# First weights fetched from ScalarE's queue, padded unit rows, weight decode in four steps, and a new order of the first ten units

## The chip, the cores and the metric

One NeuronCore of a Trainium2 chip runs the whole kernel. The metric is the device time of one execution in microseconds; lower is better. Before the change, three runs took 793.53, 794.27 and 796.66 us, a median of 794.27 us.

## What the kernel computes

Three stages follow each other. The first is a linear attention with a decaying state (batch 4, 8 heads, 768 steps, head size 48):

```python
for t in range(S):
    cur = np.einsum('bhd,bhe->bhde', u[None] * kt, vt)
    y[:, :, t] = np.einsum('bhd,bhde->bhe', rt, state + cur)
    state = wt[:, :, :, None] * state + np.einsum('bhd,bhe->bhde', kt, vt)
```

Its output is read as 3072 tokens of 384 numbers. The second stage is a dense layer with a softmax gate and a norm; the third a dense layer with a leaky maximum:

```python
h = x @ w_in                                   # 384 -> 1024
solu = h * softmax(h)
ln = (solu - mean) / sqrt(var + 1e-6) * g_ln
x = ln @ w_out                                 # 1024 -> 384
g = max(0.01 * h2, h2), h2 = x @ w2_in         # 384 -> 2048
out = g @ w2_out                               # 2048 -> 384
```

The four weight matrices and the norm's gain arrive as 64-bit floats; the attention's inputs are rounded to 32 bits on the host, which also lays them out.

## The kernel before

The 3072 tokens are cut into 24 **units** of 128 tokens. For each unit the attention is done chunk-wise: VectorE (DVE in the profile) makes running products of the decay with two scans (`prep1`, L379, into `suf`; `prep3`, L397, into `e`), scales the transposed keys and queries (`prep_k` L390 gives `kt`, `prep4` L406 gives `lt`), and TensorE (PE) makes the products (`att_scores` L447, `att_u` L467, `att_y` L510 and L519). `att_x` (L525, L526) sums the result on DVE, `x_t` transposes it, `x_hi` on ScalarE (ACT) and `x_lo` (L540) on DVE split it into a rounded high part and a low rest. `mm1` (L548) multiplies it by `w_in` in three passes of nine matmuls in each half. `soft_max` (L553, the row maximum), `soft_e`, `soft_z`, `soft_nm`, `soft_c`, `soft_q` and `z_t`, `z_hi`, `z_lo` make the gated vector and split it. `mm2` (L601) multiplies by `w_out`, four units behind.

Each unit has two tiles from memory: `tr` (112 rows of 1545 floats: decay, keys, queries; two buffers, so the fetch for unit i waits until unit i-2 is used up) and `natq` with `natv` (keys, queries and values by token). All are fetched by SyncE's queue (SP), in program order. A fetch whose buffer isn't free yet therefore holds up all that stand behind it.

Before `mm1` of unit 0 can run, the 64-bit `w_in` must be **decoded** into two 32-bit matrices. It is cut into six blocks of 128 by 512 (three rows of blocks in two halves), and `w_out` into eight of 128 by 384. For each block, `w1_a` takes the exponent (DVE, L111, then ACT, L113), and `w1_b` does four DVE instructions in a row: sign (L119), top bits (L121), sum (L123), product (L125). `w1_c` rounds the block on ACT (L671) and subtracts on PE (L673, L674, through the one PSUM tile `PO`); `w1_d` copies the rest from `PO` on ACT (L680). `w1_c` and `w1_d` of successive blocks share `PO` and so follow each other. The blocks of `w_in` are staged in the buffers `zh` (first half) and `zl` (second half) by `load_i`, and those of `w_out` by `load_o` in the second buffer of each name.

The order of all this is written out by hand: a table `FIRST` names every step of units 0 to 9 and of the decode, in the order in which the steps are issued, and each engine takes its own instructions in that order. From unit 10 on, a loop table `LOOP` repeats for each unit. After the units, the third stage runs (L763, L787). Its weights are decoded in the last part of the units and after them.

Of the kernel before, what the change touches and what calls it, by code (L numbers as in the profile page):

```python
# [35 lines left out]
prep1 2; att_mid 1; prep_diag 1; prep2 2; att_evac_s 1; att_mul_next 1; att_state 1; w1_a; prep_state 2; prep_k 2;
prep3 2; load_i 1; prep_check 1; w1_b; w1_a; att_kt 2; prep4 2; w1_a; w1_c; w1_d; w1_b; w1_c; w1_a; w1_b; w1_d;
w1_c; w1_a; load_o 0; w1_d; mm1 0 0; w1_a; prep_vd 1; w1_b; w1_c; load_tr 3; prep_check 2; w1_d; load_tr 4; w1_b;
att_y 1; load_nat 2; prep_bonus 2; w1_c; w1_b; w1_d; w1_a; w1_a; w1_c; w1_a; w1_a; w1_d; w1_b; w1_b; mm1 0 1; prep1
3; att_evac_k 2; soft_max 0; att_x 1; x_t 1; att_u 2; w1_b; soft_e 0; att_scores 2; w1_c; x_hi 1; att_mid 2; soft_z  # L40
0; soft_nm 0; prep_check 3; load_o 1; w1_d; att_evac_s 2; soft_c 0; soft_q 0; x_lo 1; prep2 3; att_mul_next 2; prep3
3; mm1 1 0; w1_c; w1_d; w1_c; w1_b; w1_a; w1_a; w1_d; prep_k 3; z_t 0; prep4 3; w1_b; load_nat 3; z_hi 0 0; att_kt
3; prep1 4; mm1 1 1; att_evac_k 3; z_lo 0 0; z_hi 0 1; prep_diag 2; prep_vd 2; w1_c; z_lo 0 1; att_state 2; att_y 2;
soft_max 1; load_tr 5; att_u 3; att_x 2; att_scores 3; w1_d; prep_bonus 3; soft_e 1; x_t 2; w1_c; load_nat 4; prep_k
4; att_mid 3; soft_z 1; x_hi 2; prep_check 4; prep_bonus 4; x_lo 2; att_kt 4; att_mul_next 3; soft_nm 1; mm1 2 0;
w1_d; soft_c 1; att_evac_s 3; prep2 4; prep3 4; w1_a; w1_b; prep4 4; mm1 2 1; z_t 1; soft_q 1; z_hi 1 0; w1_b;
att_evac_k 4; prep_diag 3; att_state 3; prep_state 3; z_lo 1 0; w1_c; z_hi 1 1; z_lo 1 1; prep_vd 3; att_scores 4;
prep_state 4; prep_check 5; att_u 4; att_y 3; soft_max 2; prep1 5; w1_d; prep_state 5; att_x 3; w1_c; soft_e 2;
soft_z 2; prep_k 5; x_t 3; att_kt 5; soft_nm 2; x_hi 3; x_lo 3; mm1 3 0; prep2 5; soft_c 2; w1_d; prep3 5; w1_a; z_t
2; att_evac_s 4; mm1 3 1; prep_diag 4; w1_b; z_hi 2 0; att_mid 4; load_nat 5; z_lo 2 0; att_evac_k 5; z_hi 2 1;  # L50
prep4 5; att_mul_next 4; z_lo 2 1; w1_c; load_tr 6; att_scores 5; prep_check 6; load_tr 7; w1_d; att_state 4;
prep_bonus 5; load_nat 6; soft_max 3; prep1 6; att_y 4; prep2 6; prep_vd 4; att_x 4; prep_diag 5; att_u 5; mm2a 4;
soft_q 2; soft_e 3; att_evac_s 5; soft_z 3; prep_state 6; prep_k 6; att_mid 5; x_t 4; x_hi 4; x_lo 4; soft_nm 3;
mm2b 4; prep_bonus 6; prep3 6; att_mul_next 5; att_state 5; mm1 4 0; prep_vd 5; mm2_out 4; soft_c 3; att_kt 6; prep4
6; z_t 3; soft_q 3; mm1 4 1; z_hi 3 0; load_nat 7; load_tr 8; z_hi 3 1; z_lo 3 0; att_scores 6; z_lo 3 1; att_evac_k
6; soft_max 4; att_u 6; att_y 5; prep_diag 6; prep_bonus 7; att_mid 6; att_mul_next 6; prep1 7; mm2a 5; att_x 5;
soft_e 4; att_evac_s 6; x_t 5; prep_k 7; prep2 7; mm2b 5; prep_check 7; soft_z 4; prep1 8; soft_nm 4; x_hi 5; x_lo
5; soft_c 4; mm1 5 0; z_t 4; prep3 7; att_kt 7; z_hi 4 0; prep4 7; prep_diag 7; prep_k 8; mm1 5 1; z_lo 4 0; z_hi 4
1; att_scores 7; prep_vd 6; prep2 8; att_state 6; z_lo 4 1; prep_vd 7; att_y 6; att_evac_k 7; soft_max 5; soft_q 4;
mm2_out 5; prep_check 8; att_u 7; prep3 8; att_kt 8; load_nat 8; att_x 6; soft_e 5; soft_z 5; x_t 6; prep_state 7;  # L60
x_hi 6; soft_nm 5; soft_c 5; mm2a 6; att_mid 7; att_evac_k 8; x_lo 6; mm1 6 0; att_mul_next 7; prep_state 8; z_t 5;
mm2b 6; load_tr 9; z_hi 5 0; z_hi 5 1; load_nat 9; prep1 9; att_state 7; mm2_out 6; z_lo 5 0; att_evac_s 7; mm1 6 1;
prep4 8; prep_check 9; soft_q 5; z_lo 5 1; soft_max 6; prep_bonus 8; att_y 7; soft_e 6; att_scores 8; att_u 8;
prep_diag 8; att_x 7; prep_k 9; prep_bonus 9; att_kt 9; soft_z 6; prep2 9; load_tr 10; soft_nm 6; prep3 9; x_t 7;
x_hi 7; mm2a 7; soft_c 6; x_lo 7; att_mid 8; prep_diag 9; mm1 7 0; prep_vd 8; prep_vd 9; soft_q 6; load_nat 10;
prep4 9; att_mul_next 8; z_t 6; z_hi 6 0; att_evac_k 9; att_evac_s 8; z_lo 6 0; mm1 7 1; prep1 10; prep_k 10; z_hi 6
1; mm2b 7; att_kt 10; z_lo 6 1; soft_max 7; soft_e 7; prep_state 9; prep2 10; att_y 8; prep_bonus 10; att_state 8;
soft_z 7; soft_nm 7; att_scores 9; att_x 8; att_u 9; att_mid 9; load_tr 11; x_t 8; prep_check 10; mm2_out 7; soft_c
7; prep3 10; x_hi 8; x_lo 8; mm2a 8; mm1 8 0; att_mul_next 9; z_t 7; prep_diag 10; prep4 10; z_hi 7 0; soft_q 7; mm1
8 1; att_evac_k 10; prep1 11; prep_state 10; z_hi 7 1; prep_k 11; prep2 11; mm2b 8; att_evac_s 9; z_lo 7 0; z_lo 7  # L70
1; att_state 9; att_scores 10; soft_max 8; att_y 9; load_nat 11; mm2_out 8; att_x 9; att_u 10; soft_e 8; att_kt 11;
x_t 9; x_hi 9; att_evac_k 11; soft_z 8; mm2a 9; soft_nm 8; x_lo 9; prep_bonus 11; mm1 9 0; soft_c 8; att_mid 10;
prep_vd 10; prep_check 11; att_mul_next 10; load_tr 12; att_evac_s 10; load_nat 12; z_t 8; prep_diag 11; z_hi 8 0;
prep1 12; prep_vd 11; prep_state 11; mm1 9 1; prep_check 12; prep_k 12; prep3 11; soft_q 8; prep_bonus 12; att_state
10; z_lo 8 0; z_hi 8 1; prep4 11; z_lo 8 1; mm2b 9; load_tr 13; mm2_out 9; prep2 12
# [39 lines left out]

def decode_val(nc, q, t, dst, scale=2.0 ** -20):
    dve = nc.vector
    hw, lw = q[:, :, 1], q[:, :, 0]
    dve.scalar_tensor_tensor(out=t, in0=hw, scalar=-2147483648, in1=t,  # L119
                             op0=ALU.bitwise_and, op1=ALU.bitwise_or)  # L120
    dve.tensor_scalar(out=hw, in0=hw, scalar1=0xFFFFF, scalar2=0x100000,  # L121
                      op0=ALU.bitwise_and, op1=ALU.bitwise_or)
    dve.scalar_tensor_tensor(out=f(lw), in0=lw.bitcast(U32), scalar=2.0 ** -32, in1=hw,  # L123
                             op0=ALU.mult, op1=ALU.add)
    dve.scalar_tensor_tensor(out=dst, in0=f(lw), scalar=scale, in1=f(t),  # L125
                             op0=ALU.mult, op1=ALU.mult)
# [898 lines left out]
```

## Time and profile before

| | |
|---|---|
| median of three runs | 794.27 us |
| the profiled execution | 794.06 us |
| its span in the trace | 792.4 us |
| PE busy | 735.5 us (93%) |
| DVE busy | 524.3 us (66%) |
| ACT busy | 355.4 us (45%) |
| POOL busy | 166.2 us (21%) |

The busy shares are means over stages of different kinds. The chain of work that ended last gives 65% of the span to PE and 22% to DVE. The span in 40 slices, of 19.8 us each, shows where PE is not full: in the first nine slices, and again around 340 to 500 us, where the third stage's weights are decoded.

### The profile page before, as it was taken

The numbers are of one execution on the slowest core, as the hardware profiler recorded it, in microseconds if no ns is written. First come the engines' busy times: TensorE is split into PE (matmuls) and PEld (weight loads), VectorE is DVE, ScalarE is ACT, GpSimd is POOL, SyncE is SP. The second block draws the span as 40 slices with busy tenths as digits, with TensorE's granted clock in tenths as the row PEclk, the third lists the DMA queues.
The fourth block names the chain that finished last, engine by engine and source line by source line (L and its number), as shares of the span: only waits on it lengthen the run. The fifth ranks groups of instructions, "written<-read, shape, count | busy, mean of one in ns | idle before, by whom it ended". The sixth has DMA issues, their size and how long they took to land.

```text
span 792.4 us, 14979 instructions
## 1 busy us (share of the span) xinstructions
PE 735.5 (93%) x6197; PEld 614.0 (77%) x6197; DVE 524.3 (66%) x866; ACT 355.4 (45%) x648; POOL 166.2 (21%) x181
## 2 busy tenths in 40 slices
...
GB/s 198 251 176 66 67 141 113 145 76 152 134 93 180 118 161 87 12 81 130 91 129 169 80 81 60 1 122 39 0 1 81 0 1 41 0 1 41 0 1 43
DMA packets 31261, 66.60 MB, mean 84 GB/s; under 512 B 4188, under 2 KB 16628, under 8 KB 31060
## 3 DMA queue, kind: packets, MB, share of 16 engines
...
## 4 chain that ended last, share of the span: by engine, by line
PE 65%; DVE 22%; ACT 4%; DMA 4%; issue 3%; POOL 1%; SPq 0%; DVEq 0%; ACTq 0%; POOLq 0%
PE acc L787 19%; PE h L763 18%; PE PH L548 9%; PE PO L601 9%; DMA tr<-in_trw_dram 2%; DVE t L771 2%; PE PZ L510 2%; PE PZ L578 2%; ACT gh L772 2%; DVE w2s L123 2%; DVE w2t L119 2%; DVE gw L777 1%; DVE w2s L121 1%; PE PA L447 1%; PE PZ L519 1%
## 5 line engine op out<-in xcount | busy, mean ns | idle before, releaser
L771 DVE TENSOR_TENSOR t<-t,h 128x512 f32<-128x512 f32 x96 | 65.8, 686 | 122.1 <-ACT t L770 122.1
L763 PE MATMUL h<-x2h,w2ih 128*128 128x512 f32 x288 | 114.5, 397 | 8.1 <-DVE t L771 8.0
L770 ACT ACTIVATE t<-h 128x512 f32<-128x512 f32 x96 | 57.3, 597 | 134.7 <-PE h L763 134.7
L777 DVE TENSOR_TENSOR gw<-t,gh 128x512 fp32r<-128x512 f32 x96 | 69.4, 723 | 66.2 <-ACT gh L772 66.2
L787 PE MATMUL acc<-gh,w2oh 128*128 128x512 f32 x288 | 113.0, 392 | 0.0
L787 PE MATMUL acc<-gw,w2oh 128*128 128x512 f32 x288 | 112.6, 391 | 0.0
L787 PE MATMUL acc<-gh,w2ol 128*128 128x512 f32 x288 | 112.5, 391 | 0.0
L763 PE MATMUL h<-x2l,w2ih 128*128 128x512 f32 x288 | 112.4, 390 | 0.0
L763 PE MATMUL h<-x2h,w2il 128*128 128x512 f32 x288 | 112.2, 390 | 0.0
L772 ACT CAST gh<-t 128x512 fp32r<-128x512 f32 x96 | 59.9, 624 | 95.3 <-DVE t L771 95.3
L754 POOL TENSOR_TENSOR x2l<-x2l,x2h 128x1536 fp32r<-128x1536 f32 x4 | 14.0, 3506 | 297.8 <-ACT x2h L750 297.8
L763 PEld LDWEIGHTS h<-x2h,w2ih 128*128 128x128 f32 x288 | 54.0, 188 | 27.4 <-DVE t L771 16.6
L787 PEld LDWEIGHTS acc<-gh,w2oh 128*128 128x128 f32 x288 | 54.5, 189 | 11.5
L787 PEld LDWEIGHTS acc<-gw,w2oh 128*128 128x128 f32 x288 | 54.5, 189 | 11.3
L787 PEld LDWEIGHTS acc<-gh,w2ol 128*128 128x128 f32 x288 | 54.4, 189 | 11.4
L763 PEld LDWEIGHTS h<-x2h,w2il 128*128 128x128 f32 x288 | 54.1, 188 | 11.5
L763 PEld LDWEIGHTS h<-x2l,w2ih 128*128 128x128 f32 x288 | 54.1, 188 | 10.6
L601 PE MATMUL PO<-zh,w1oh 128*128 128x384 f32 x168 | 59.7, 355 | 0.0
L548 PE MATMUL PH<-w1ih,xh 128*128 128x512 f32 x144 | 58.5, 406 | 0.6 <-ACT junk L373 0.6
L548 PE MATMUL PH<-w1ih,xl 128*128 128x512 f32 x144 | 56.9, 395 | 0.2 <-DVE xl L540 0.2
L548 PE MATMUL PH<-w1il,xh 128*128 128x512 f32 x144 | 56.5, 392 | 0.0
L601 PE MATMUL PO<-zh,w1ol 128*128 128x384 f32 x168 | 56.5, 336 | 0.0
...
## 6 DMA issues: line engine op xcount, KB each, us to landing
...
```

What stands on the lines that cost most here:

```text
L119: dve.scalar_tensor_tensor(out=t, in0=hw, scalar=-2147483648, in1=t, op0=ALU.bitwise_and, op1=ALU.bitwise_or)
L123: dve.scalar_tensor_tensor(out=f(lw), in0=lw.bitcast(U32), scalar=2.0 ** -32, in1=hw, op0=ALU.mult, op1=ALU.add)
L510: pe.matmul(out=y[64 * c:64 * c + 64, hs], lhsT=s[64 * c:64 * c + 64, x, q], rhs=a[64 * c:64 * c + 64, h], start=(h == 0), stop=False, ski ...
L548: pe.matmul(out=PH[:, half], lhsT=a[:, kc], rhs=c[:, kc, 512 * half:512 * half + 512], start=(n == 0), stop=(n == 8))
L578: pe.transpose(PZ[c // 4][:, 128 * (c % 4):128 * (c % 4) + 128], zbuf[:, 128 * c:128 * c + 128], ident)
L601: pe.matmul(out=o2[m], lhsT=a[:, c, 128 * m:128 * m + 128], rhs=d[:, c], start=(c == 0 and q == 0), stop=(c == K1 - 1 and q == 2))
L763: pe.matmul(out=h2, lhsT=a[:, kc, 128 * o:128 * o + 128], rhs=d[:, kc], start=(q == 0), stop=(q == 8))
L770: act.activation(out=t, in_=h2, func=AF.Copy, scale=0.01)
L771: dve.tensor_tensor(out=t, in0=t, in1=h2, op=ALU.max)
L772: act.copy(out=gh, in_=t)
L777: dve.tensor_tensor(out=gw, in0=t, in1=f(gh), op=ALU.subtract)
L787: pe.matmul(out=at, lhsT=a[:, c % 4, 128 * o:128 * o + 128], rhs=d, start=(c == 0 and q == 0), stop=(c == K2 - 1 and q == 2))
```

## The change

1. `w_in` is no longer fetched by `load_i` from SP's queue in the middle of `FIRST`. A new `load_w1` issues it from ACT's queue, right after the issue of unit 0's `tr`, in three transfers: first half block row 0, first half block rows 1 and 2, and the whole second half.
2. `tr` rows are padded in memory from 1545 to 1600 floats (the tile and the bytes moved are as before), `nat` is split into two arrays (`nat_q`, `nat_v`), and these transfers are declared as integers. Unit 0's `tr` comes in two pieces in place of three. The gain `g_ln` is laid out by the host so that each of 128 rows reads 32 bytes in a row.
3. The four DVE instructions of `w1_b` become four steps (`w1_e` sign, `w1_f` top bits, `w1_h` sum, `w1_b` product) that the table can place apart. The instructions are the same.
4. The table `FIRST` is written anew for units 0 to 9. It ends in the same state; `LOOP` and all behind it are as before.

```diff
-def body(tc, trw, nat, w1p, u_p, r, k, v, w, u, w1i, w1o, gln, w2i, w2o, out):
+def body(tc, trw, nat_q, nat_v, w1p, u_p, g_p, r, k, v, w, u, w1i, w1o, gln, w2i, w2o, out):
...
             for a, b in zip(cuts, cuts[1:]):
-                eng.dma_start(out=t[0:112, a:b], in_=trw[i, 0:112, a:b])
+                eng.dma_start(out=t[0:112, a:b].bitcast(I32), in_=trw[i, 0:112, a:b].bitcast(I32))
...
-            eng.dma_start(out=q, in_=nat[i, :, 1:3])
-            eng.dma_start(out=t, in_=nat[i, :, 0])
+            eng.dma_start(out=q.bitcast(I32), in_=nat_q[i].bitcast(I32))
+            eng.dma_start(out=t.bitcast(I32), in_=nat_v[i].bitcast(I32))
...
-        def load_i(hf):
-            t = ma.tile([128, K1 * 384], I32, name="zl" if hf else "zh")
-            for kc in range(KC):
-                q = t[:, 1024 * kc:1024 * kc + 1024]
-                sp.dma_start(out=q, in_=w1p.bitcast(I32)[128 * kc:128 * kc + 128, 1024 * hf:1024 * hf + 1024])
-                stage["i", kc, hf] = q.rearrange("p (n c) -> p n c", c=2)
+        def load_w1():
+            for hf in range(2):
+                t = ma.tile([128, K1 * 384], I32, name="zl" if hf else "zh")
+                for a, n in ((0, 1), (1, 2)) if hf == 0 else ((0, 3),):
+                    act.dma_start(
+                        out=t[:, 1024 * a:1024 * (a + n)].rearrange("p (k n) -> p k n", k=n),
+                        in_=w1p.bitcast(I32)[128 * a:128 * (a + n), 1024 * hf:1024 * hf + 1024]
+                        .rearrange("(k p) n -> p k n", p=128),
+                    )
+                for kc in range(KC):
+                    stage["i", kc, hf] = t[:, 1024 * kc:1024 * kc + 1024].rearrange("p (n c) -> p n c", c=2)
...
-            sp.dma_start(out=gl, in_=gln.rearrange("(k p) -> p k", p=128))
+            sp.dma_start(out=gl, in_=g_p)
...
-        def w1_b():
-            if not w1_run:
+        w1_step = [w1_run, [], [], []]
+
+        def w1_b(n):
+            if not w1_step[n]:
                 return
-            key, q, t = w1_run.pop(0)
-            x = f(q[:, :, 0])
-            if key[0] == "i":
-                decode_val(nc, q, t, x)
+            key, q, t = w1_step[n].pop(0)
+            if n == 0:
+                decode_sign(nc, q, t)
+            elif n == 1:
+                decode_top(nc, q)
+            elif n == 2:
+                decode_sum(nc, q)
             else:
-                decode_val(nc, q, t, x, gl[:, key[1]:key[1] + 1])
-            w1_done.append((key, x))
+                x = f(q[:, :, 0])
+                decode_mul(nc, q, t, x, 2.0 ** -20 if key[0] == "i" else gl[:, key[1]:key[1] + 1])
+                w1_done.append((key, x))
+                return
+            w1_step[n + 1].append((key, q, t))
...
-            load_tr(0, sp, (0, 521, 1033, TRW))
+            load_tr(0, sp, (0, 521, TRW))
+            load_w1()
...
-prep1 0; load_u; prep_check 0; load_nat 0; prep2 0; prep_state 0; prep3 0; load_tr 1; prep_k 0; load_nat 1; prep4 0;
+load_tr 1; prep1 0; prep2 0; w1_a; load_nat 0; prep3 0; prep_k 0; w1_e; load_u; w1_f; prep4 0; att_scores 0; w1_a;
...
```

**DVE at the program's start.** The first rows on DVE before the change, from unit 2's first scan (line 379) to the first decoded block; `ebuf` is the scratch of the exponent and `zh` the staged block, lines 111 and 119 to 125 are the decode. Ahead of these stand all of units 0 and 1 but for a few steps:

```order
21 L379 SCALAR_TENSOR_TENSOR suf<-tr,sel 112x520
22 L427 TENSOR_REDUCE dg<-natq 128x8
23 L385 RECIPROCAL e_112<-suf 112x8
24 L456 COPY_PREDICATED ss_122<-mask,PA 128x512
25 L491 TENSOR_TENSOR st_118<-PA,ao 112x192
26 L111 TENSOR_SCALAR ebuf<-zh 128x512
27 L390 TENSOR_TENSOR kt<-tr,suf 112x512
28 L397 SCALAR_TENSOR_TENSOR e_327<-tr,e_112 112x520
29 L119 SCALAR_TENSOR_TENSOR ebuf<-zh,ebuf 128x512
30 L121 TENSOR_SCALAR zh<-zh 128x512
31 L123 SCALAR_TENSOR_TENSOR zh<-zh 128x512
32 L125 SCALAR_TENSOR_TENSOR zh<-zh,ebuf 128x512
```

On DVE at the same place of the program's start, now (the scans are lines 397 and 415, the decode lines 114 and 120 to 136):

```order
5 L397 SCALAR_TENSOR_TENSOR suf<-tr,sel 112x520
6 L403 RECIPROCAL e_112<-suf 112x8
7 L114 TENSOR_SCALAR ebuf<-zh 128x512
8 L415 SCALAR_TENSOR_TENSOR e_164<-tr,e_112 112x520
9 L408 TENSOR_TENSOR kt<-tr,suf 112x512
10 L120 SCALAR_TENSOR_TENSOR ebuf<-zh,ebuf 128x512
11 L125 TENSOR_SCALAR zh<-zh 128x512
12 L424 TENSOR_TENSOR lt<-tr,e_164 112x512
13 L114 TENSOR_SCALAR ebuf<-zh 128x512
14 L114 TENSOR_SCALAR zbuf<-zh 128x512
15 L131 SCALAR_TENSOR_TENSOR zh<-zh 128x512
16 L120 SCALAR_TENSOR_TENSOR ebuf<-zh,ebuf 128x512
```

The first block's exponent moved from DVE's row 26 to row 7, between the scans of unit 0, and the blocks two and three to rows 13 and 14.

**SP's queue, units 4 to 7.** SP's rows before the change, from unit 5's `tr` on; the two `tr` of row 26 and 27 are units 6 and 7, and `natq`, `natv` behind them are unit 6's:

```order
21 L361 DMA tr_657<-in_trw_dram 112x1545
22 L367 DMA natq_705<-in_nat_dram 128x768
23 L368 DMA natv_704<-in_nat_dram 128x384
24 L367 DMA natq_922<-in_nat_dram 128x768
25 L368 DMA natv_921<-in_nat_dram 128x384
26 L361 DMA tr_936<-in_trw_dram 112x1545
27 L361 DMA tr_956<-in_trw_dram 112x1545
28 L367 DMA natq_963<-in_nat_dram 128x768
29 L368 DMA natv_962<-in_nat_dram 128x384
```

SP's rows now, from unit 5's `tr` (row 21) on:

```order
21 L379 DMA tr_636<-in_trw_dram 112x1545
22 L385 DMA natq_764<-in_nat_q_dram 128x768
23 L386 DMA natv_763<-in_nat_v_dram 128x384
24 L379 DMA tr_925<-in_trw_dram 112x1545
25 L385 DMA natq_932<-in_nat_q_dram 128x768
26 L386 DMA natv_931<-in_nat_v_dram 128x384
27 L379 DMA tr_1035<-in_trw_dram 112x1545
```

Unit 6's `natq` and `natv` (rows 25 and 26) now stand ahead of unit 7's `tr` (row 27) and no longer behind it.

## Rows read from the trace of the kernel before

**Rows 1.** The page's first part: busy time of each engine.

```profile
PE 735.5 (93%) x6197; PEld 614.0 (77%) x6197; DVE 524.3 (66%) x866; ACT 355.4 (45%) x648; POOL 166.2 (21%) x181
```

**Rows 2.** Stretches up to the row maxima of units 0, 4 and 9.

```profile
core 0: us, PE busy (x) PEld busy (x) DVE busy (x) ACT busy (x) POOL busy (x), PEclk, DMA share, GB/s
0.00:54.55 54.55, 28.48 (x279) 17.84 (x279) 43.28 (x73) 21.86 (x43) 12.62 (x27) 0.99 0.78 226
54.55:112.41 57.86, 49.88 (x687) 38.78 (x689) 54.42 (x92) 37.80 (x75) 21.04 (x27) 0.95 0.28 87
112.41:180.69 68.28, 64.24 (x908) 57.08 (x905) 54.75 (x83) 38.10 (x74) 35.21 (x38) 1.00 0.38 104
```

**Rows 3.** The chain that ended last: start us, us, what.

```profile
32.46 0.60 ACT w1il L680
...
35.64 0.60 ACT w1il L680
...
98.47 6.80 DMA natq<-in_nat_dram
...
182.07 2.31 PE PO L601 x12
...
194.63 2.31 PE PO L601 x12
```

**Rows 4.** DVE in order of time: start us, us, instruction [idle before <-releaser].

```profile
3.70 1.24 DVE L379 TENSOR_TENSOR_SCAN suf<-tr,sel 112x520 f32<-112x520 f32 x1 [1.51 <-DMA tr<-in_trw_dram]
...
13.53 0.55 DVE L427 TENSOR_REDUCE dg<-natq 128x8 f32<-128x384 f32 x1 [3.84 <-POOL natq L423]
...
24.31 0.42 DVE L111 TENSOR_SCALAR ebuf<-zh 128x512 int32<-128x512 int32 x1
...
26.40 0.67 DVE L119 SCALAR_TENSOR_TENSOR ebuf<-zh,ebuf 128x512 int32<-128x512 int32 x1
27.10 0.43 DVE L121 TENSOR_SCALAR zh<-zh 128x512 int32<-128x512 int32 x1
...
28.29 0.69 DVE L125 SCALAR_TENSOR_TENSOR zh<-zh,ebuf 128x512 f32<-128x512 f32 x1
...
53.35 1.20 DVE L553 TENSOR_REDUCE nmax<-PH 128x1 f32<-128x1024 f32 x1
...
108.78 0.36 DVE L491 TENSOR_TENSOR st<-PA,ao 112x192 f32<-112x192 f32 x1 [1.32 <-POOL ao L486]
...
111.20 1.21 DVE L553 TENSOR_REDUCE nmax<-PH 128x1 f32<-128x1024 f32 x1
...
133.56 1.24 DVE L379 TENSOR_TENSOR_SCAN suf<-tr,sel 112x520 f32<-112x520 f32 x1 [2.54 <-DMA tr<-in_trw_dram]
```

**Rows 5.** SP's queue in order of time: start us, us of issue, transfer.

```profile
7.72 3.50 SPq L361 DMA_DIRECT2D tr<-in_trw_dram  x1
11.26 1.63 SPq L616 DMA_DIRECT2D zh<-in_w1p_dram  x3
14.84 3.96 SPq L616 DMA_DIRECT2D zl<-in_w1p_dram  x3
...
85.06 13.32 SPq L361 DMA_DIRECT2D tr<-in_trw_dram  x2
...
125.62 0.35 SPq L361 DMA_DIRECT2D tr<-in_trw_dram  x1
```

**Rows 6.** Transfers issued from 2 to 20 us: count, KB each, median us to landing.

```profile
zh<-in_w1p_dram SPq DMA_DIRECT2D x3, 512.0 KB, 11.9
...
gl<-in_moe_g_ln_dram SPq DMA_DIRECT2D x1, 4.0 KB, 12.4
```

**Rows 7.** The early stretches in which transfers run, same columns as rows 2.

```profile
2.00:12.00 10.00, 2.07 (x36) 1.60 (x36) 4.78 (x7) 2.66 (x8) 2.22 (x9) 1.00 0.93 231
12.00:20.00 8.00, 5.04 (x89) 4.48 (x89) 5.93 (x9) 0.85 (x2) 3.85 (x6) 1.00 1.07 205
20.00:30.00 10.00, 4.19 (x71) 2.95 (x70) 9.34 (x17) 3.69 (x8) 2.89 (x4) 1.00 1.02 387
```

More of the change, by code (lines that the diff above doesn't have):

```diff
@@ L36 @@
[L36 to L75, printed above, removed]
+load_tr 1; prep1 0; prep2 0; w1_a; load_nat 0; prep3 0; prep_k 0; w1_e; load_u; w1_f; prep4 0; att_scores 0; w1_a;
@@ new lines @@
+mm1 1 0; w1_e; prep_state 3; w1_b; load_nat 4; w1_e; z_t 0; w1_f; prep_check 3; att_scores 2; w1_f; w1_c; w1_a;
+w1_h; w1_h; w1_d; prep1 4; w1_b; mm1 1 1; z_hi 0 0; att_evac_s 2; z_hi 0 1; att_evac_k 3; w1_c; prep4 3; att_u 3;
+w1_d; z_lo 0 0; z_lo 0 1; soft_q 0; prep_state 4; att_mid 3; soft_max 1; w1_e; att_mul_next 3; load_tr 5; w1_b;
+prep2 4; prep_bonus 3; att_y 2; soft_e 1; w1_c; att_x 2; soft_z 1; x_t 2; att_state 3; soft_nm 1; prep_diag 3;
+att_scores 3; x_hi 2; w1_a; w1_d; w1_f; w1_a; x_lo 2; soft_c 1; w1_e; soft_q 1; w1_h; prep_k 4; w1_b; prep3 4; mm1 2
@@ new lines @@
+att_mid 7; load_tr 9; soft_z 5; prep_bonus 8; x_hi 6; soft_nm 5; load_nat 9; soft_c 5; x_lo 6; prep3 8; mm2b 6;
+prep4 8; mm2_out 6; att_mul_next 7; prep1 9; prep_vd 7; mm1 6 0; z_t 5; mm1 6 1; prep2 9; att_state 7; z_hi 5 0;
+att_kt 8; z_lo 5 0; z_hi 5 1; mm2a 7; load_tr 10; z_lo 5 1; prep_diag 8; prep_k 9; att_evac_k 8; soft_max 6; att_y
+7; att_u 8; load_nat 10; soft_q 5; prep_state 8; prep3 9; att_scores 8; att_kt 9; att_x 7; soft_e 6; x_t 7; att_mid
+8; prep_bonus 9; x_hi 7; prep4 9; soft_z 6; prep_state 9; x_lo 7; mm2b 7; att_evac_k 9; mm1 7 0; att_mul_next 8;
@@ new lines @@
+7 1; mm1 8 1; att_state 9; soft_max 8; mm2_out 8; prep_state 10; load_tr 12; soft_q 7; soft_e 8; att_scores 10;
+att_y 9; att_x 9; soft_z 8; prep2 11; att_u 10; att_evac_s 10; prep3 11; prep_vd 10; soft_nm 8; mm2a 9; soft_c 8;
+att_mid 10; x_t 9; x_hi 9; load_nat 12; x_lo 9; prep_diag 11; mm2b 9; prep_check 11; att_mul_next 10; z_t 8; mm1 9
+0; z_hi 8 0; z_lo 8 0; prep1 12; prep4 11; z_hi 8 1; prep_k 12; att_kt 11; mm2_out 9; att_evac_k 11; z_lo 8 1;
+prep_vd 11; prep_check 12; prep_bonus 12; mm1 9 1; prep_state 11; att_state 10; soft_q 8; prep2 12; load_tr 13
```

82 lines of the change are left out of this document (59 added, 23 removed).

## The prediction

> **What bounds the kernel now.** I read the busy times first: PE is busy for 93% of the span and every other engine for less [rows 1]. So time can only be gained where PE is not full. The stretches cut at three marks, the ends of the row maxima (`soft_max`) of units 0, 4 and 9, say which engine holds it up [rows 2]. Up to 54.55 us PE is busy for 28.5 us, DVE for 43.3. From there to 112.41 us DVE is busy for 54.4 of 57.9 us: it is the bound, and waits for only 3.4. From 112.41 to 180.69 us PE is busy for 64.2 of 68.3 us, DVE for 54.8. Behind that, the loop is bound by PE: the same `mm2` stands at 182.07 and 194.63 on the chain [rows 3], 12.56 us for each unit. The change ends where the loop begins, in the same state. What it gains or loses up to unit 9's row maximum, the whole kernel gains or loses; the loop and the third stage keep their length.
>
> So the sum has three stretches:
> - Stretch 1, 0 to 54.55: DVE idle 54.55 - 43.28 = 11.3 us.
> - Stretch 2, 57.9 us: DVE idle 3.4 us.
> - Stretch 3, 68.3 us, for five units: the floor is 5 x 12.56 = 62.8 us of PE's work, so 5.5 us are lost.
>
> **Where stretch 1 loses its time.** DVE's first scan runs at 3.70, when the first piece of `tr` has landed; up to there some 2.6 us were idle (3.70 less about 1.1 of its own clearing). It waits 3.84 us at 13.53 for unit 0's bonus, which waits for `natq`. The first block's decode starts at 24.31 [rows 4]. SP could not issue the fetch of `w_in` before 11.26, because unit 2's `tr` stood ahead and held SP for 3.50 us, and the first three of its six transfers took about 11.9 us each to land [rows 5, 6].
>
> **Part by part.**
>
> *The decode in four steps.* The four instructions are the same, 0.67, 0.43, about 0.69 and 0.69 us [rows 4]. Cost nothing; the cover is DVE itself, in order. Should the pieces stand badly, a piece costs its wait, which the stretches below count.
>
> *The fetch from ACT's queue.* Three issues ahead of ACT's first work. SP's issues took about 0.5 us each where they did not wait, 1.63 for three [rows 5], so ACT is late by some 1.5 us, at a time when its first real work, the first exponent, is not due before 6 us. Nothing. What counts is when the bytes land. By 20 us the transfers filled the engines: share 0.93 and 1.07, at 231 and 205 GB/s; from 20 to 30 us it was 387 [rows 7]. The slow stretch held the gain's 4 KB, which took 12.4 us to land [rows 6] for 1024 pieces of four bytes; that transfer now comes later and in rows. The fast stretch was almost all weights, in rows of 3 and 4 KB. The new beginning mixes both kinds, so I take the mean of 231 and 387, 309 GB/s, and keep both ends. Two queues share it, half each. Then the first block (524 KB) lands at 2.2 + 3.4 + 0.5 = 6.1 us (2.2 is when data begins to flow, 0.5 the tail to the semaphore, both estimated from the first `tr` piece, issued at 0.81 and there by 3.7), blocks two and three at 12.9, the second half at 23.1.
>
> The Trainium skill, page "DMA: Bandwidth & Descriptors", section "Issuing engines are not separate DMA queues", says that transfers of all issuing engines run on the same 16 DMA engines and interleave, so that a second issuer saves only issue time. It speaks against this part: if the second queue brought its own 309 GB/s, the last weights would land at 12.9 and no wait for them would be left, a gain of 6 us in stretch 1 and a sum of 784.3; by the rule, it is the half-and-half above. The shares of 0.93 and 1.07 under one queue agree with the rule.
>
> *DVE's new order, walked through.* First scan at 4.2, half a microsecond later, because the weights take half the rate; start idle 3.1. Scan and reciprocal to 5.5; wait 0.6 for the first block. Exponent, scan, `kt`, sign, top bits, `lt`: 0.42 + 1.24 + 0.67 + 0.67 + 0.43 + 0.69 = 4.1, to 10.2; wait 2.7 for blocks two and three, since DVE's next instructions are their exponents. Rows 13 to 26 of its order are 9.9 us (two exponents, two signs, two top bits, three sums, three products, two scans, a reciprocal), to 22.8; wait 0.3 for the second half. From there DVE has no transfer to wait for. But ACT takes the exponents of the second half ahead of unit 0's `ks` copy, and each block goes through `PO` in about 3.2 us (32.46 to 35.64 [rows 3]); with five blocks to go after the first and ACT's copies for the attention between them, I get the last `w1il` about 1.2 us after DVE could use it. Short gaps, as now, 1.0. Idle: 3.1 + 0.6 + 2.7 + 0.3 + 1.2 + 1.0 = 8.9. DVE's work up to the mark is the same: it has one top-bits step, one sum and two products less (0.4 + 0.6 + 1.2) and one `kt`, one state update and unit 1's two sums into `x` more (0.7 + 0.4 + 1.1). Stretch 1: 11.3 - 8.9 = **2.4 us gained**.
>
> The bounds: at 387 GB/s the landings are 5.4, 10.8 and 18.9, the waits for weights shrink to 1.2 in all, idle 6.5, gain 4.8. At 231 the landings are 7.2, 16.3 and 29.9, the waits 1.7, 5.0 and 3.7, idle 15.7: a loss of 4.4.
>
> *Stretch 2.* DVE is full, so only its idle and its work count. It waits 1.32 us at 108.78 for POOL, which waited for unit 6's `natq`: 6.80 us on the chain from 98.47 [rows 3, 4]. That transfer stood behind unit 7's `tr`, for whose buffer SP waited up to 98.4 (13.32 us for two issues from 85.06 [rows 5]). In the new order `natq` stands ahead of that `tr`, so this wait goes. Against that one scan and one reciprocal (1.4 us) of a later unit now stand ahead of unit 4's row maximum. **0 gained**; between -3 (new waits as large as those that there are) and +3.4 (none left).
>
> *Stretch 3.* Here PE is nearly full. DVE's wait of 2.54 us at 133.56 is for unit 9's `tr`, issued at 125.62 [rows 4, 5], because on SP it stood behind the output of an `mm2`. In the new order 25 DVE instructions, some 17 us, lie between unit 7's `lt`, which frees the buffer, and unit 9's scan; one landing fits in. This wait goes, and 1.4 us of DVE's work were done before. What is late next is PE itself: 62.8. With the 2.5 alone it is 65.7; I take the middle between that and the floor, 64.3. **4.0 gained**, between 0 (another wait comes up) and 5.5.
>
> *Padding, integers, split arrays, one piece of `tr` less.* The same bytes into the same tiles. DVE waits for a `tr` twice of note, at the start and the 2.54; both are counted. Nothing; bounds -0.5 to +0.5 (the start's `tr` alone is waited for).
>
> **Sum.** 2.4 + 0 + 4.0 = 6.4. The profiled execution took 794.06 us (span 792.4 and 1.7 around it), 0.2 below the median of 794.27. Median after: 794.27 - 6.4 = **787.9 us**. About 0.5%, 4 us, is what a measurement here can tell from no change: below 790.3 is faster, above 798.2 slower.
>
> **Rivals.**
>
> *All three stretches near their bounds.* Weights at 387 GB/s, 4.8; a microsecond from stretch 2; PE full from unit 4 on, 5.5. That is 11.3 in all: 783.0 us. For it: PE has work enough from unit 4 on, and the 4 KB rows ran that fast. Against it: unit 0's and 1's own rows (6 KB, 3 KB, 1.5 KB) come between, and they never did better than 231 in a mixed stretch.
>
> *The fetch gains nothing, or the waits only move.* At 231 GB/s stretch 1 loses 4.4 and stretch 3 gives it back: 794.7. Or stretch 1 gains 2.4 and PE's stretch nothing, since another late input takes the place of the `tr`: 791.9. For it: DVE's work is not reduced anywhere, and the transfers were at their limit up to 30 us already. Against it: DVE has the first weights some 18 us earlier (6.1 for 24.31), as filler for its waits.
>
> *Slower: unit 0's attention is tied to the second half of the weights.* ACT works in order, and its copy of unit 0's keys (`ks`) now stands behind the three exponents of the second half, so all of units 0 and 1 waits for the last of 3 MB. Before, no step of unit 0's attention stood behind the weights. Place: ACT, at the second half's landing. At 205 GB/s the landings are 7.8, 18.0 and 33.4, the idle 19.2 instead of 11.3, a loss of 7.9; with the 2.5 of the `tr` given back, 799.7 us. From 282 GB/s down (by a straight line between the idle at 309 and at 231) stretch 1 is a loss, and from about 210 the whole is slower by more than 0.5%. For it: 205 is what the trace shows for 12 to 20 us. Against it: that stretch held the 4-byte pieces.
>
> **How the numbers follow.** Forecast 0.40, with its own range 784 to 790.3; the better case 0.20; the two forms of no change 0.27; slower 0.13. That gives faster 0.60, same 0.27, slower 0.13. The range that should hold 8 in 10 reaches to 780.5 on one side, past the better case by 2.5, and to 796 on the other, which takes in both forms of no change and leaves the worst of the slow case out.
>
> **What would show it.** In the changed kernel's trace: the weights' three transfers land near 6, 13 and 23 us; DVE shows idle time ahead of the exponents of block two, 2 to 3 us; `ks` of unit 0 on ACT at 25 to 27 us; unit 0's row maximum ends near 52, unit 4's near 110, unit 9's near 174; no wait of DVE on `natq` or on a `tr` from unit 6 on; the distance of the row maxima from unit 9 on is 12.56 as before. I am wrong in stretch 1 if the second half lands after 27 us or before 20, in stretch 3 if the five units take more than 66 us, and altogether if the loop's period changes.

## The result and the profile after

The changed kernel takes 783.87 us, the median of 4 runs (783.24 to 785.48), beside 794.33 for the kernel before in the same session (4 runs, 793.53 to 796.66). The ratio is 0.9867, 95% interval 0.9841 to 0.9892: 10.5 us less. The profiled execution took 783.52 us with a span of 781.8, before 792.4.

The page's first part, after. Against [rows 1] DVE lost 5.8 us of busy time with the same 866 instructions.

```profile
PE 730.4 (93%) x6197; PEld 612.9 (78%) x6197; DVE 518.5 (66%) x866; ACT 354.2 (45%) x648; POOL 162.6 (21%) x181
```

The same three stretches as [rows 2], up to the row maxima of units 0, 4 and 9, same columns:

```profile
0.00:49.72 49.72, 26.00 (x318) 16.96 (x318) 41.80 (x74) 22.25 (x45) 14.25 (x27) 1.00 0.67 223
49.72:106.39 56.67, 49.43 (x639) 39.22 (x640) 52.61 (x93) 36.81 (x73) 21.79 (x27) 0.97 0.38 108
106.39:169.19 62.80, 61.30 (x939) 54.86 (x933) 52.39 (x81) 38.11 (x74) 28.22 (x37) 1.00 0.43 127
```

Against [rows 2] they are 4.83, 1.19 and 5.48 us shorter, 11.5 in all. The ten units behind the third mark take 125.6 us, before 125.8. The span fell by 10.6 only; the last output's transfer took about 1 us longer to land in this execution, which I can't explain.

DVE in order of time, after; these rows answer to [rows 4]:

```profile
5.60 1.24 DVE L397 TENSOR_TENSOR_SCAN suf<-tr,sel 112x520 f32<-112x520 f32 x1 [3.42 <-DMA tr<-in_trw_dram]
...
7.00 0.38 DVE L114 TENSOR_SCALAR ebuf<-zh 128x512 int32<-128x512 int32 x1
...
13.62 0.43 DVE L114 TENSOR_SCALAR ebuf<-zh 128x512 int32<-128x512 int32 x1 [2.50 <-DMA zh<-in_w1p_dram]
...
14.30 0.69 DVE L131 SCALAR_TENSOR_TENSOR zh<-zh 128x512 f32<-128x512 uint32 x1
14.90 0.68 DVE L120 SCALAR_TENSOR_TENSOR ebuf<-zh,ebuf 128x512 int32<-128x512 int32 x1
15.50 1.48 DVE L120 SCALAR_TENSOR_TENSOR zbuf<-zh,zbuf 128x512 int32<-128x512 int32 x1
...
23.74 0.40 DVE L114 TENSOR_SCALAR zbuf<-zl 128x512 int32<-128x512 int32 x1
...
48.51 1.21 DVE L571 TENSOR_REDUCE nmax<-PH 128x1 f32<-128x1024 f32 x1
...
105.17 1.22 DVE L571 TENSOR_REDUCE nmax<-PH 128x1 f32<-128x1024 f32 x1 [0.57 <-PE PH L566]
```

Read two things here. The first exponent runs at 7.00 instead of 24.31 [rows 4]. And an instruction that stands behind a stranger, one whose result it does not read, starts 0.60 us after it (14.30, 14.90, 15.50). In [rows 4] the four steps of one block, each reading the result of the one before, start 0.70, 0.46 and 0.73 apart (26.40, 27.10, 27.56, 28.29). The third of them, before the change:

```profile
27.56 0.69 DVE L123 SCALAR_TENSOR_TENSOR zh<-zh 128x512 f32<-128x512 uint32 x1
```

The weights' transfers, issued at 0.80 to 2.24 us: KB each and us to landing; then the rates of [rows 7] again; then unit 0's `ks` on ACT.

```profile
zl<-in_w1p_dram ACTq DMA_DIRECT2D x1, 1536.0 KB, 17.7
zh<-in_w1p_dram ACTq DMA_DIRECT2D x1, 1024.0 KB, 12.3
...
zh<-in_w1p_dram ACTq DMA_DIRECT2D x1, 512.0 KB, 5.3
...
2.00:12.00 10.00, 0.83 (x32) 0.83 (x32) 5.40 (x9) 2.41 (x4) 1.63 (x8) 1.00 0.99 287
12.00:20.00 8.00, 3.60 (x19) 1.61 (x13) 6.38 (x11) 3.55 (x7) 2.25 (x2) 1.00 1.03 393
20.00:30.00 10.00, 3.56 (x37) 2.08 (x37) 9.59 (x19) 3.73 (x7) 3.29 (x4) 1.00 0.65 215
...
26.02 0.51 ACT L471 COPY ks<-PK 128x448 f32<-128x448 f32 x1
```

So they land at 6.1, 13.6 (where DVE's wait ends) and 19.9 us.

### The profile page after: what moved, and what is told of

Read it like the earlier page. It is cut to its first block, busy times and chain, and to the rows that moved or that the text cites. A ratio compares the mean times of both kernels' runs of the same rounds, so it can differ in the third digit from the quotient of the medians.

```text
span 781.8 us, 14968 instructions
## 1 busy us (share of the span) xinstructions
PE 730.4 (93%) x6197; PEld 612.9 (78%) x6197; DVE 518.5 (66%) x866; ACT 354.2 (45%) x648; POOL 162.6 (21%) x181
## 3 DMA queue, kind: packets, MB, share of 16 engines
q10 hardware_dynamic: 816, 3.15, 1.2%
## 4 chain that ended last, share of the span: by engine, by line
PE 72%; DVE 18%; issue 4%; ACT 3%; DMA 2%; POOL 0%; DVEq 0%; ACTq 0%; POOLq 0%
PE acc L818 18%; PE h L794 18%; PE PH L566 12%; PE PO L619 11%; PE PZ L596 3%; PE PZ L528 2%; DVE t L802 2%; ACT gh L803 2%; DVE w2s L131 2%; DVE w2t L120 2%; DMA ub<-in_u_p_dram 2%; PE PZ L537 1%; PE PA L465 1%; DVE gw L808 1%; DVE w2s L125 1%
## 5 line engine op out<-in xcount | busy, mean ns | idle before, releaser
L794 PEld LDWEIGHTS h<-x2h,w2il 128*128 128x128 f32 x288 | 54.4, 189 | 11.5
```

The lines of the kernel that those rows point to most:

```text
L794: pe.matmul(out=h2, lhsT=a[:, kc, 128 * o:128 * o + 128], rhs=d[:, kc], start=(q == 0), stop=(q == 8))
```

## Experiments

My theory after the result (S): the decode's steps, apart from each other, save DVE about 0.36 us for each of 14 blocks, 5 us, beside what the order gives. Its rivals: the order alone (O), the early fetch alone (F), the queue that fetches (Q). The letters of later expectations are explained in them.

**The four steps joined again**, at the place of the product, all else as changed:

```diff
-w1_e=lambda: w1_b(0), w1_f=lambda: w1_b(1), w1_h=lambda: w1_b(2), w1_b=lambda: w1_b(3)
+w1_e=lambda: None, w1_f=lambda: None, w1_h=lambda: None, w1_b=lambda: [w1_b(n) for n in range(4)]
```

> The changed kernel with the four decode steps joined again at the place of the product step; fetch, padding and the rest of the order as changed. Theory S (the gain that the prediction missed is the split: a decode instruction that needs the one before it starts 0.70, 0.46, 0.73 us after it, and 0.60, 0.34, 0.60 when another stands between, some 0.36 us a block, 14 blocks, 5 us, of which the first two stretches, bound by DVE, keep nearly all): 3.5 to 5 us above the changed kernel, 787.5 to 789, unit 0's row maximum some 2 us later and the decode instructions stepping at 0.70/0.46/0.73. Theory O (the order and the early weights bring it all, the split nothing): 783.9 within 1.

Measured: 796.86 us, ratio to before 1.0034 (1.0021 to 1.0047), 13.0 more than the changed kernel. Both theories missed. Its first two stretches, and DVE's largest waits for other engines up to 112 us (who for whom: us in all, times, longest), then the same two waits after:

```profile
0.00:57.32 57.32, 27.49 (x318) 17.66 (x318) 40.86 (x70) 22.25 (x45) 13.42 (x27) 0.94 0.58 193
57.32:120.49 63.17, 54.01 (x637) 43.63 (x639) 57.84 (x96) 37.00 (x73) 21.55 (x27) 0.86 0.33 97
...
DVE x L543 <- PE PZ L537: 4.5, 3, 1.9
DVE st L509 <- POOL ao L504: 4.0, 2, 2.2
...
DVE x L543 <- PE PZ L537: 0.9, 3, 0.4
...
DVE st L509 <- POOL ao L504: 0.4, 1, 0.4
```

Stretches 1 and 2 are 7.6 and 6.5 us longer than after, the third, 62.86, is not. DVE waits 4.5 and 4.0 us for the attention's PE and POOL (after: 0.9 and 0.4). In this order the three earlier steps were what DVE did while it waited; joined, they come in one piece of 2.5 us, and delay the attention's next step as well. S holds for the work itself: DVE's busy time over the whole kernel is 522.9 us, so that 4.4 of the 5.8 us which the change took away are back.

The lower granted clock has a part in the 13.0. It is 0.94 and 0.86 in these stretches (after: 1.00 and 0.97), and PE is busy for 81.5 us in them instead of 75.4 with nearly the same matmuls. It is not the whole: in the last kernel below it is 0.89 and 0.86, and unit 4's row maximum ends at 109.37 us, here at 120.49. How much of the 13.0 it is, no run shows; nor was the decode joined at an earlier place.

**The early fetch alone**, in the kernel before:

```diff
 load_tr(0, sp, (0, 521, 1033, TRW))
+load_w1()                    # the three transfers from ACT's queue
-load_i=load_i
+load_i=lambda hf: None
```

> The kernel before with one thing changed: w_in fetched at the start from ACT's queue, as in the changed kernel; the old order, decode in one piece, old input layout. Theory S and the order (the early weights are worth nothing while the decode stands behind units 0 and 1 in DVE's row): 794 to 797, the first decode instruction still near 24 us or later, and the first scan near 5.6 in place of 3.7. Theory F (the late weights were the wait, the early fetch by itself brings the gain of the first stretch): about 789, decode beginning before 20 us.

Measured: 800.98 us, ratio 1.0089 (1.0072 to 1.0106): slower. Its first stretch, and its first exponent:

```profile
0.00:59.94 59.94, 28.71 (x279) 18.01 (x279) 42.42 (x73) 21.70 (x43) 13.08 (x27) 0.99 0.65 206
...
29.49 0.42 DVE L111 TENSOR_SCALAR ebuf<-zh 128x512 int32<-128x512 int32 x1
```

The weights are there, but the order asks for them only behind unit 2's attention, and 3 MB more in the first 20 us make the inputs of units 0 to 2 late (DVE waits 6.1 us for `tr`, before 1.9): the first exponent comes at 29.49, 5.2 us later than in [rows 4], and the stretch is 5.4 longer. The third stretch is 68.27 as before.

**The same transfers from SP's queue**, all else as changed:

```diff
-act.dma_start(
+sp.dma_start(
     out=t[:, 1024 * a:1024 * (a + n)]...
```

> The changed kernel with the three weight transfers issued from SP's queue at the same place of the program, so that unit 1's tr, unit 0's natq and natv stand behind 3 MB in one queue. Theory Q (the second queue is what brings the early weights without holding up the units' inputs): 2 to 4 us slower than the changed kernel, 786 to 788, DVE waiting for unit 1's tr or for POOL on natq. Theory N (one engine pool, the place in the program counts and not the queue): first scan back near 3.7, blocks two and three at 10 to 11 us in place of 13.3, 782 to 784.

Measured: 786.15 us, ratio 0.9896 (0.988 to 0.9913), 2.3 more than after, though the intervals of the two overlap. The trace says where: stretch 1 is 2.8 us longer (52.50), the next two are as after (56.73 and 62.81). That is Q. DVE's scans of units 0 and 1:

```profile
3.66 1.24 DVE L397 TENSOR_TENSOR_SCAN suf<-tr,sel 112x520 f32<-112x520 f32 x1 [1.48 <-DMA tr<-in_trw_dram]
...
20.88 1.24 DVE L397 TENSOR_TENSOR_SCAN suf<-tr,sel 112x520 f32<-112x520 f32 x1 [4.72 <-DMA tr<-in_trw_dram]
```

On one queue the first `tr` comes 1.9 us sooner, and unit 1's `tr`, issued behind 3 MB, so late that DVE waits 4.72 us for it; after, the scan at 18.78 waited for nothing. Not run: one queue with unit 1's inputs ahead of the weights.

**Rows not padded, floats instead of integers**, all else as changed:

```diff
-TRP = 1600
+TRP = TRW                    # and no .bitcast(I32) in load_tr and load_nat
```

> The changed kernel with tr rows of 1545 floats again and all unit inputs declared as floats. My theory (the padding and the integers change nothing that anyone waits for): 783.9 within 1. Rival (padded rows are what raised the early rate from 231 to 287 GB/s): the first scan or the exponents of blocks two and three 1 to 2 us later, 785 to 786.

Measured: 786.22 us (783.10 to 788.04), ratio 0.9891 (0.9863 to 0.992), an interval that overlaps that of the changed kernel: not told apart. Unit 0's row maximum is 0.4 us later, in its first three waits; the other 2.2 us of this execution arise between units 0 and 3, where the run with unit 6's `natq` moved, below, loses the same beside a lower granted clock.

**Two blocks' steps in turns, in the kernel before**, which takes the dependent starts away and leaves the order (the edit in short):

```diff
+def decode_pair(nc, blocks):  # sign A, sign B, top A, top B, sum A, sum B, product A, product B
 def w1_b():
-    (one block)
+    (two blocks where two are ready; the next call then does nothing)
```

> The kernel before, with one part: where two blocks' exponents are ready, the four decode instructions of both are issued in turns (sign of A, sign of B, top bits of A, top bits of B, and so on), so that no instruction stands right behind the one whose result it reads. Fetch and order of all else are those of before. Theory S (a dependent instruction right behind its source starts about 0.1 us later, some 0.36 us for each block): 12 of 14 blocks are paired, 4.3 us of DVE's time, about 2.2 in each of the first two stretches, of which DVE bounds the second wholly: 790 to 792, and the rows of the paired blocks step 0.60, 0.34, 0.60, 0.60. Theory O (the order and the landing alone make the gain): 794, no change.

Measured: 793.79 us (10 runs, 792.08 to 798.73), ratio 0.9998 (0.9978 to 1.0018): no change, against the time that S expects. A pair's first steps on DVE, and its largest wait up to 112 us:

```profile
37.17 0.69 DVE L117 SCALAR_TENSOR_TENSOR w2s<-zl,w2s 128x512 int32<-128x512 int32 x1 [1.97 <-ACT w2s L113]
37.78 0.76 DVE L122 TENSOR_SCALAR zl<-zl 128x512 int32<-128x512 int32 x2
38.45 1.29 DVE L128 SCALAR_TENSOR_TENSOR zl<-zl 128x512 f32<-128x512 uint32 x2
...
DVE w2s L117 <- ACT w2s L113: 5.1, 3, 2.0
```

The pair does step by 0.60 and 0.34, as S says, and DVE is busy for 3.2 us less (521.1 for 524.3), but it is then early for ACT's part of the exponent and waits 5.1 us for it (before: 1.9). The time saved becomes another wait.

**Two blocks in turns in the changed order**, as the first experiment, in pairs. The gain is loaded beside `u`. The pair multiplies the first block of `w_out` by the gain before the gain has its factor of 2^-20, so that block's values are too large; the instructions are the same.

```diff
-w1_b=lambda: [w1_b(n) for n in range(4)]
+w1_b=w1_b                     # decode_pair; load_u; load_g
```

> The changed kernel with the four steps joined at the product's place as in the first experiment (796.9), but two blocks at a time, in turns; the gain is loaded earlier, beside u, since the pair needs it. Theory S: the 0.36 us of each of 12 blocks come back, 4 us: 792 to 793. Theory O (it is the place of the steps, as work for DVE's waits, that counts, and joined steps hold DVE up): no better than 796 to 798, since a pair blocks DVE for twice as long.

Measured: 795.90 us, ratio 1.0017 (1.0003 to 1.0031): 1.0 less than joined singly, 12 more than apart. DVE is busy for 3.6 us less up to unit 4's row maximum (95.1 for 98.7), but waits 5.8 us for `PZ` and 4.0 for `ao`. On balance S gives back 1 us of the 13. That is no bound on it, since a pair also holds DVE for twice as long. O, in the form that the place of the steps counts, fits the rest, by elimination.

**More work on DVE in stretch 2**, and, in another kernel, in stretch 3:

```diff
+if 0 <= i < 4:                # the other kernel: 4 <= i < 8
+    for _ in range(2):
+        dve.tensor_reduce(out=anyf, in_=flat(sel), axis=AX.X, op=ALU.max)
```

> The changed kernel with two more reductions on DVE (0.6 us each, result not used, estimated from the row maximum's 1.2 us for twice the elements) behind the exponential's correction of units 0 to 3: 8 instructions, some 4.8 us, all in stretch 2. Theory D (DVE bounds stretch 2, 52.6 of 56.7 us busy): 3.5 to 4.8 slower, 787.5 to 788.7, and stretch 3 unchanged at 62.8. Theory P (by now PE and the transfers bound it, DVE has slack): at most 1 slower, 783.9 to 785.

> The changed kernel with two more reductions on DVE (1.42 us a pair by the run that added them to units 0 to 3; result not used) behind the exponential's correction of units 4 to 7, 5.7 us, all in stretch 3. Theory P (PE alone bounds stretch 3): 62.8 again, at most 1 slower, 784 to 785. Theory D (DVE is near its limit there too): 3 to 5.7 slower, 787 to 789.5.

Measured: 790.58 us (ratio 0.995, 0.9933 to 0.9967) and 785.54 (0.9869, 0.9842 to 0.9897). A pair took 1.42 us, four of them 5.7. Stretches 2 and 3 of the first kernel:

```profile
50.04:113.12 63.08, 52.07 (x639) 40.93 (x641) 57.76 (x101) 36.94 (x73) 21.83 (x27) 0.92 0.33 97
113.12:175.92 62.80, 61.32 (x939) 54.88 (x932) 52.40 (x81) 38.10 (x74) 28.30 (x37) 1.00 0.44 128
```

And of the second:

```profile
49.41:108.02 58.61, 51.58 (x638) 41.57 (x639) 52.58 (x92) 36.76 (x73) 21.57 (x27) 0.91 0.35 105
108.02:173.07 65.05, 62.14 (x939) 54.66 (x932) 55.97 (x90) 38.10 (x74) 27.26 (x37) 1.00 0.41 123
```

In stretch 2 most or all of the 5.7 us shows: it is 6.4 longer than after, and 4.2 longer than in the two experiments with nearly the same granted clock there (0.91: 58.88 and 58.83, rows not padded and unit 6's `natq` moved). DVE bounds it. In stretch 3 2.3 us shows (65.05 against 62.80): PE bounds it, with some 3.5 us of slack on DVE, less than I expected.

**Unit 6's `natq` behind unit 7's `tr`** again, all else as changed:

```diff
-w1_c; load_nat 6; att_u 5; ... load_tr 7; prep_bonus 5;
+w1_c; att_u 5; ... load_tr 7; load_nat 6; prep_bonus 5;
```

> The changed kernel with one transfer moved: unit 6's natq and natv are issued behind unit 7's tr, as before, instead of ahead of it. Theory N (natq of unit 6 behind that tr was what DVE waited for in stretch 2): a wait of 1 to 1.5 us for POOL or natq comes back near unit 4's row maximum: 785 to 785.5. Theory F (from there on PE has the time to make it good, stretch 3 at its floor anyhow or the transfer in time): 783.9.

Measured: 785.49 us (784.52 to 786.58), ratio 0.9889 (0.9867 to 0.9911). The number is N's, the trace does not bear N out: `natq` goes out at 93.14, behind a `tr` that SP held for its buffer, no wait for it comes back, and from unit 3's row maximum to unit 4's it is 11.66 us (after: 11.68). What the execution lost, 2.2 us, it lost between units 0 and 3, where nothing was moved. PE there, in this kernel (the number ahead of the DMA share is the granted clock):

```profile
54.00:58.00 4.00, 4.00 (x14) 3.22 (x14) 4.00 (x9) 2.62 (x7) 0.20 (x1) 0.50 0.69 240
...
78.00:82.00 4.00, 3.66 (x106) 3.47 (x107) 3.36 (x5) 2.57 (x5) 3.01 (x4) 0.63 0.61 177
```

and in the changed kernel:

```profile
54.00:58.00 4.00, 4.00 (x48) 3.19 (x47) 4.00 (x9) 2.46 (x6) 0.36 (x1) 0.73 0.67 237
...
78.00:82.00 4.00, 3.85 (x96) 3.20 (x89) 3.62 (x7) 2.14 (x4) 3.92 (x6) 1.00 0.52 157
```

Half the clock (1.2 of 2.4 GHz) for longer at the first place, and at the second at all: 1.1 us each, by the row maxima around them (13.84 us for 12.73 from unit 0 to 1, 15.95 for 14.91 from 2 to 3). The execution without padding had 0.68 at the second place too. So no effect under 2 us can be read from one execution in this stretch. And `natq`, though behind that `tr` again, goes out 15.6 us ahead of the end of unit 4's row maximum, before 13.9.

**Unit 9's `tr` ahead of the output of the `mm2`**, in the kernel before:

```diff
-mm2_out 5; ... mm2b 6; load_tr 9; z_hi 5 0;
+load_tr 9; mm2_out 5; ... mm2b 6; z_hi 5 0;
```

> The kernel before with one transfer moved: unit 9's tr is issued ahead of the output of an mm2 (where its buffer comes free at 122.0 us, the end of unit 7's lt) instead of behind it at 125.62, 3.6 us earlier. Theory T (that tr's wait of 2.54 us is what stretch 3 loses): the wait goes and the stretch falls by about 2.5, 68.3 to 65.8, the time to 791.5 to 792. Theory C (the stretch is short of time through the chain of attention and mm1 that the order makes, the wait lies beside others that end as late): the wait goes or shrinks, another takes its place, 68 and 794.

Measured: 794.73 us (10 runs), ratio 1.0006 (0.9989 to 1.0023), which is C. Its third stretch, and DVE where the wait was:

```profile
112.26:180.56 68.30, 64.39 (x916) 57.22 (x913) 55.63 (x83) 38.05 (x74) 36.09 (x38) 1.00 0.35 104
...
131.04 2.51 DVE L379 TENSOR_TENSOR_SCAN suf<-tr,sel 112x520 f32<-112x520 f32 x1 [0.17 <-POOL ao L486]
...
138.87 1.23 DVE L553 TENSOR_REDUCE nmax<-PH 128x1 f32<-128x1024 f32 x1 [1.24 <-PE PH L548]
```

The 2.54 us of [rows 4] are gone and the stretch is as long as it was: the scan, now beside POOL's work on `natq`, takes 2.51 us instead of 1.24, and what it still gained is gone when the next row maximum waits 1.24 us for PE (before: 0.82).

**A version to beat both**: the first block's sum and product in DVE's wait of 2.50 us, the first half in three transfers; and the same with unit 2's scores ahead of unit 1's `mm1`, in PE's idle time:

```diff
-att_scores 0; w1_a; w1_a; w1_h; w1_e; prep_state 0; w1_e; w1_b;
+att_scores 0; w1_h; w1_b; w1_a; w1_a; w1_e; prep_state 0; w1_e;
-for a, n in ((0, 1), (1, 2)) if hf == 0
+for a, n in ((0, 1), (1, 1), (2, 1)) if hf == 0
-mm1 1 0; ... prep_check 3; att_scores 2;      # the second kernel
+att_scores 2; mm1 1 0; ... prep_check 3;
```

> The changed kernel with the first block's sum and product put ahead of the exponents of blocks two and three, into DVE's wait of 2.50 us at 13.62, and the first half fetched in three transfers, so that block two's exponent need not wait for block three. If the wait is idle time that the start can use: 1.2 us from the two steps and up to 1 from block two's earlier landing, 781.8 to 782.7, and unit 0's row maximum near 46.5 to 47.3 instead of 48.5. If the start is held by what lands last (the second half of the weights and unit 1's tr): 783.9, row maximum at 48.5.

> The same, and unit 2's scores matmuls put ahead of unit 1's first expert matmul, into PE's idle time of 3.35 us at 49.16 behind unit 0's expert matmuls. In the changed kernel's run PE then stood at a granted clock of 0.5 from about 52.5 to 56 us, in the runs of the experiments to 59 or 60. If that idle time brings the clock down: with 0.5 us of work in its middle the low stretch goes or shortens, 1 to 2 us less than without it, 780 to 782. If not: the same as without it within 0.5 us.

Measured: 783.50 us (781.77 to 784.32), ratio 0.986 (0.9843 to 0.9876), and 783.46 (0.9853, 0.9837 to 0.987). Both medians are 0.4 us below the changed kernel's and not told apart from it; the gains expected were missed. In the traces the first idea works: DVE in the first kernel,

```profile
11.65 0.69 DVE L131 SCALAR_TENSOR_TENSOR zh<-zh 128x512 f32<-128x512 uint32 x1
12.37 0.69 DVE L136 SCALAR_TENSOR_TENSOR zh<-zh,ebuf 128x512 f32<-128x512 f32 x1
...
13.71 0.43 DVE L114 TENSOR_SCALAR zbuf<-zh 128x512 int32<-128x512 int32 x1 [0.32 <-DMA zh<-in_w1p_dram]
```

and unit 0's row maximum is at 47.30, 1.2 us earlier. The second does not: the scores run at 47.74, at the beginning of the idle time and not in its middle, so that it only shrinks to 2.77 us (after: 3.35), and the clock is halved behind it all the same. Whether work in its middle would keep the clock up stays open. Its row on PE, the same row after (52.51), and the stretch in this kernel:

```profile
51.21 0.79 PE L566 MATMUL PH<-w1ih,xh 128*128 128x512 f32 x1 [2.77 <-DVE zbuf L578]
...
52.51 0.64 PE L566 MATMUL PH<-w1ih,xh 128*128 128x512 f32 x1 [3.35 <-DVE zbuf L578]
...
52.00:54.00 2.00, 2.00 (x7) 1.61 (x6) 2.00 (x6) 1.97 (x4) 0.00 (x0) 0.50 1.01 251
```

## Why the prediction was right, and where not

Its time, 787.9, is 4.0 above the 783.87 measured. That is inside the range that was to hold 8 in 10 (780.5 to 796), but 0.1 below the forecast's own 784 to 790.3, in the better case that had 0.20. Faster was its likeliest verdict. By its steps:

*What bounds the kernel.* Right: of 5.7 us of work added to DVE most or all shows in stretch 2, 2.3 in stretch 3, and the period from unit 9 on is unchanged.

*Stretch 1, 2.4 predicted, 4.83 measured.* Two terms of the sum were mis-sized. DVE's idle: 8.9 predicted, 7.9 measured (49.72 less 41.80). The start cost 4.5 instead of 3.1 (the first scan at 5.60, not 4.2), blocks two and three 2.50 as foretold (2.7), and the waits for the first block, the second half and `PO`, 2.1 together (0.1 less if scan and reciprocal, 1.24 and 0.21 us from 4.2, end at 5.65 and not at 5.5), did not come: the transfers ran at 287 and then 393 GB/s, not at an even 309 (the weights were 3.15 of the 6.03 MB up to 20 us, near the half that I took), so the second half was there at 19.9 instead of 23.1, just outside the bound that I set for being right. The gain's 4-byte pieces are not shown to be what slowed the early stretch: in the kernel with the fetch alone they took 12.7 us to land, and the rate from 12 to 20 us was 317. And "DVE's work up to the mark is the same": it fell by 1.5. That the steps no longer stand right behind what they read is the likely reason, since 4.4 us of busy time came back with the joined steps; no run shows it for this stretch alone.

*"Cost nothing", on the decode in four steps.* This is the step that failed most, for it hid a gain. Joined in the same order, the kernel takes 13.0 us more. The dependent starts themselves gave little (in pairs: nothing in the old order, 1.0 in the new). The rows show instead that the pieces are what DVE does while the attention's PE and POOL are at work, and that PE, kept waiting, then runs at a lower clock.

*The fetch from ACT's queue.* Alone it costs 7.0 us (800.98 against 794.03 in its session). The new order asks for the first weights at 7.00 us, when the old fetch had not been issued yet (11.26 [rows 5]); that it belongs to the gain there is argued from that, and no run has the new order with the old fetch. The Trainium skill ("DMA: Bandwidth & Descriptors", "Issuing engines are not separate DMA queues") lets a second issuer save issue time only. The trace agrees on the bandwidth, as the prediction took it: the DMA share is 0.99 and 1.03 with two queues, as it was with one [rows 7]. But the second queue was worth 2.3 us here, against the same order of issue on one queue, through the order of landing: its weights no longer stand ahead of unit 1's `tr`.

*Stretch 2, 0 predicted, 1.19 measured.* Inside its bounds. That `natq`'s wait goes is right; its place in SP's queue is not what does it, for put back, it brings no wait in the new order.

*Stretch 3, 4.0 predicted, 5.48 measured.* Near in size, wrong in mechanism. "This wait goes [...] With the 2.5 alone it is 65.7": it can be taken away in the kernel before, and the stretch stays at 68.30. It was a wait of DVE in a stretch that PE bounds. The view to read was who PE waits for; before, in stretch 3:

```profile
PE PZ L500 <- DVE zl L591: 2.2, 3, 1.0
PE PZ L531 <- DVE x L526: 1.6, 3, 0.8
```

and after:

```profile
PE PA L465 <- DVE ao L497: 1.2, 1, 1.2
PE PA L465 <- DVE lt L424: 0.3, 1, 0.3
...
100.71 0.42 PE L619 MATMUL PO<-zh,w1oh 128*128 128x384 f32 x1
...
102.71 0.33 PE L619 MATMUL PO<-zh,w1ol 128*128 128x384 f32 x1
```

PE waits 2.5 us less (1.5 for 4.0), for `zl` and `x` of DVE no more. And it has 2.9 us less to do in the stretch (61.30 for 64.24). 2.2 of them are the step `mm2a 5`, the first half of one `mm2`, 12 matmuls from 100.71 to 102.9, which stands in stretch 2 now, where PE has idle time; before, it ran from 113.40. The new order's text says so (`mm2a 5` ahead of `soft_max 4`), and I had not read it. The kernels with the new order have 62.8 to 62.9 there, but for the one with work added on DVE; those with the old order 68.2 to 68.3. That these two are the cause is read from the traces; no run moved them alone.

*The rivals.* The better case, 783.0, came out, by its landing and by PE's full stretch; in stretch 1 partly by luck, since only 3.4 of its 4.8 us came from idle time and 1.5 from DVE's work, which it took as unchanged. The slower one did not: `ks` came at 26.02, as the forecast had it. That an early fetch can make unit 0 late in another way, through its inputs, is what the fetch alone shows. *Padding, integers:* nothing, not told apart from nothing.

What stays open: how the 6.0 us of stretches 1 and 2 divide between fetch, split and order (the fetch alone lost, fetch and order without the split lost, the order and the split were not run alone); and the 1.2 of stretch 2, which is below what the clock does there.
